# An adaLN attention block on one core: four edits to the order of TensorE's work and to one sum of the tail

## The chip, the cores and the metric

The kernel runs on 1 core of one Trainium2 chip. The metric is the device time of the whole program in microseconds (us), lower is better. The engines are TensorE (PE; its weight loads are PEld), VectorE (DVE), ScalarE (ACT), GpSimd (POOL) and SyncE (SP), which issues most DMAs.

## The reference

Two batches of 256 tokens, width 1152, all bf16. A modulation vector from c scales and shifts a layer norm of x; one attention head over the full width follows; a gate and x close the block.

```python
def reference(x, c, wqkv, wo, w_mod):        # x 2x256x1152, c 2x1152
    mod = (_silu(c) @ w_mod).reshape(B, 6, 1, D)
    shift_a, scale_a, gate_a = mod[:, 0], mod[:, 1], mod[:, 2]   # the rest is unused
    h = _layernorm(x, axis=-1) * (1 + scale_a) + shift_a
    q, k, v = split(h @ wqkv, 3)
    p = _softmax(einsum('bqd,bkd->bqk', q, k) * D ** (-0.5), axis=-1)
    a = einsum('bqk,bkd->bqd', p, v) @ wo
    return x + gate_a * a
```

## The kernel before

There are T = 512 tokens in TT = 4 tiles of 128 (tiles 0 and 1 are batch 0, tiles 2 and 3 batch 1), and the width is KT = 9 blocks of 128. The order of the instructions on PE, DVE, ACT and SP's queue is the order in which the program records them: the helpers `ten`, `vec`, `sca` and `spq` note every instruction, and `pin` at the end ties each to the one before it. All of them are therefore shown under one line, L76, in the profile, and are told apart by their tiles. POOL's instructions keep program order too. PSUM has two pools: `psum` with six slots (tag "mm") and `psum_pre` with two (tag "pre"). A slot passes to the next tile of its tag when the tile in it has been read for the last time.

The stages, in order of PE's work:

1. **Start.** Eleven filler matmuls (`fillers`, tile junk_ps) run while the first loads are under way. c is turned into silu(c), repeated along columns in scT_rep. DVE and ACT normalise x (xn), PE transposes xn (`transposes(t, h)`: h = 0 is blocks 0 to 3, KA = 4 of them, h = 1 is blocks 4 to 8), and ACT or DVE copies the result to xnT (`xnT_copy`).
2. **Scale, first column part.** `scale_block` multiplies wS, the scale columns of w_mod, with silu(c), one 128-column block j of the output and one of the nine blocks kk of the input at a time. For the first KA = 4 output blocks the result lies in psSA, one PSUM bank, which a matmul of ones fills with the 1 of (1 + scale). DVE's `scaled(k, b, ...)` multiplies block k of xnT for batch b with it into hTs; s1p holds the values for later use.
3. **Half steps.** `qkv_half(k, b)` adds block k of batch b to six accumulators accs (the first 768 columns of wqkv, from wA): six matmuls of 256 columns. They stand between the transposes of tiles 3 and 2.
4. **Scale, second column part.** psSB collects the remaining five output blocks (45 matmuls of 54 columns), DVE adds 1 into s1p and makes ten scaled tiles. Then `qkv_step(4)` to `qkv_step(8)`, six matmuls of 512 columns each for both batches, with the shift blocks (wH, bankH) and a seventh accumulator between them, and the shift's part through wqkv as a bias.
5. **The other columns of Q and K**: 11 groups of nine 512-column matmuls from hT, weights wq_t. DVE meanwhile builds the gate (gacc from wG); POOL sums it over the partitions (gate_bc).
6. **Scores**, then V: `v_group(gidx)`, twelve groups of nine 384-column matmuls, each emptied into v_sb by ACT or DVE. The softmax (DVE, ACT) yields pn for each batch.
7. **P's transposes**: eight transposes into two "pre" tiles pT_ps, copied to pT by DVE (batch 0) and ACT (batch 1); then attention, 36 matmuls of 256 columns, into attnT.
8. **Output.** For each token tile, three 384-column chunks of nine matmuls with wO. DVE multiplies with gate_bc (ga) and adds x (o_sb), and SP sends the tile out. The last tile's last 384 columns are cut into 320 and 64. For them POOL has multiplied wo with the gate beforehand (wo_last, nine products, L572), and x enters through PE by an identity matmul at the head of the chunk; DVE copies the 320 columns out, ACT the 64, and ACT's queue sends these.

The loads are issued by SP in a fixed order: c, two tiles of x, wS's first part in five pieces, wA for blocks 0, 1 to 2 and 3, wS's second part in two pieces, wA for blocks 4 to 5 and 6 to 8, wH in five pieces, then the other weights. wG takes wS's place in SBUF, wO takes wH's.

Of the kernel before, what the change touches and what calls it, by code (L numbers as in the profile page):

```python
# [8 lines left out]
ALU = mybir.AluOpType  # L9
AX = mybir.AxisListType  # L10
F32 = mybir.dt.float32
# [5 lines left out]
def kernel(  # L17
# [10 lines left out]
    P = 128  # L28
    B, N, D = x.shape
    T = B * N  # L30
    KT = D // P
    TT = T // P
    NQ = N // P
    CW = 384
    NCH = D // CW
# [6 lines left out]
    KA = 4  # L42
    CA = KA * P
    NRS = 96
    NRH = 54
# [14 lines left out]
    psum_pre = ctx.enter_context(tc.tile_pool(name="psum_pre", bufs=2, space=PSUM))  # L60
# [22 lines left out]
    vec = _Rec(nc.vector, dve_seq)  # L83
    sca = _Rec(nc.scalar, act_seq)
    ten = _Rec(nc.tensor, pe_seq)

    def pin(seq):
# [11 lines left out]
        out=ident, in_=ident, compare_op=ALU.not_equal, fill=1.0, base=0,  # L99
# [4 lines left out]
    ones_bf = const.tile([P, P], BF16)  # L104
    nc.gpsimd.memset(ones_bf, 1.0)
    ones_row = const.tile([1, 512], BF16)
# [9 lines left out]
    x_sb = act.tile([P, TT, D], BF16)  # L116
# [29 lines left out]
    wS = wmpool.tile([P, KT, D], BF16, tag="wS")  # L146
# [25 lines left out]
    def fillers(n):  # L172
        for jj in range(n):
            ten.matmul(junk_ps, lhsT=ident, rhs=junk_rhs, start=True, stop=True)
# [8 lines left out]
        out=scT_f.rearrange("p k b -> p b k"),  # L183
        in0=cT_ps.rearrange("p (b k) -> p b k", b=B),
        in1=e_sb.rearrange("p (b k) -> p b k", b=B),
        op=ALU.mult,
# [4 lines left out]
    def sc_rhs(kk, n):  # L191
        return scT_rep[:, kk].rearrange("p r b -> p (r b)")[:, 0:n]
# [17 lines left out]
    def dve_norm(t):  # L210
        vec.scalar_tensor_tensor(
            out=nb[:, t : t + 1], in0=mv_all[:, t, 0:1], scalar=-1.0, in1=rstd[:, t : t + 1],
            op0=ALU.mult, op1=ALU.mult,
        )
        vec.tensor_scalar(
            out=xn[:, t, :], in0=x_sb[:, t, :], scalar1=rstd[:, t : t + 1], scalar2=nb[:, t : t + 1],
            op0=ALU.mult, op1=ALU.add,
        )
# [22 lines left out]
    def transposes(t, h, pool, tag):  # L241
        k0, k1 = HALF[h]
        tp = pool.tile([P, KH, P], BF16, tag=tag, name="tp")
        for k in range(k0, k1):
            ten.transpose(tp[:, k - k0, :], xn[:, t, k * P : (k + 1) * P], ident)
        tps[t, h] = tp

    def xnT_copy(t, h, on_dve):
        k0, k1 = HALF[h]
        dst, srct = xnT[:, k0:k1, t * P : (t + 1) * P], tps[t, h][:, : k1 - k0, :]  # L250
        if on_dve:
            vec.tensor_copy(out=dst, in_=srct)
        else:
            sca.copy(out=dst, in_=srct)


    s1p = const.tile([P, KT, B], F32)
# [1 line left out]
    sh_bf = const.tile([P, KT, B], BF16)  # L259
    hTs = act.tile([P, KT, T], BF16, tag="a3")  # L260

    psSA = psum_pre.tile([P, KA, NRS], F32, tag="pre")
    ten.matmul(psSA.rearrange("p j r -> p (j r)"), lhsT=ones_bf[0:1, :],
               rhs=ones_row[0:1, 0 : KA * NRS], start=True, stop=False, skip_group_check=True)
    fillers(N_JUNK - 6)

    def scale_block(ps_, n, k0, k1, kk, ones=True):
        for j in range(k0, k1):
            ten.matmul(
                ps_[:, j - k0, :], lhsT=wS[:, kk, j * P : (j + 1) * P], rhs=sc_rhs(kk, n),  # L270
                start=(kk == 0 and j == k0 and not ones), stop=(kk == KT - 1), skip_group_check=True,
            )

    def scaled(k, b, scalar):
        sl = slice(b * N, (b + 1) * N)
        vec.tensor_scalar(out=hTs[:, k, sl], in0=xnT[:, k, sl], scalar1=scalar, scalar2=None, op0=ALU.mult)

    def qkv_half(k, b):
        sl = slice(b * N, (b + 1) * N)
        for f in range(NACC):  # L280
            ten.matmul(
                accs[f][:, sl], lhsT=wA[:, k, f * P : (f + 1) * P], rhs=hTs[:, k, sl],
                start=(k == 0 and b == 0), stop=False, skip_group_check=True,
            )
# [30 lines left out]
    dve_norm(1)  # L315
    dve_stats(2, 0)
    dve_norm(0)
    scale_block(psSA, NRS, 0, KA, 0)
    scale_block(psSA, NRS, 0, KA, 1)
    transposes(1, 0, psum, "mm")  # L320
    transposes(1, 1, psum, "mm")
    xnT_copy(1, 0, False)
    xnT_copy(1, 1, False)
    scale_block(psSA, NRS, 0, KA, 2)
    scale_block(psSA, NRS, 0, KA, 3)
    transposes(0, 0, psum, "mm")
    transposes(0, 1, psum, "mm")
    xnT_copy(0, 0, False)
# [3 lines left out]
    dve_aggr(2)  # L332
    act_norm(3)
    for kk in range(4, KT):
        scale_block(psSA, NRS, 0, KA, kk)

    accs = []
    for f in range(NACC):
        acc_t = psum.tile([P, T], F32, tag="mm")
        accs.append(acc_t)  # L340

    scaled(0, 0, psSA[:, 0, 0:1])
    vec.tensor_copy(out=s1p[:, 0:KA, :], in_=psSA[:, :, 0:B])
    for k in range(1, KA):
        scaled(k, 0, s1p[:, k, 0:1])
    dve_norm(2)
    qkv_half(0, 0)
    qkv_half(1, 0)
    qkv_half(2, 0)
    transposes(3, 0, psum_pre, "pre")  # L350
    xnT_copy(3, 0, False)
    transposes(2, 0, psum_pre, "pre")
    xnT_copy(2, 0, True)
    qkv_half(3, 0)
    transposes(3, 1, psum_pre, "pre")
    xnT_copy(3, 1, False)
    for k in range(KA):
        scaled(k, 1, s1p[:, k, 1:2])
    for k in range(3):
        qkv_half(k, 1)  # L360
    transposes(2, 1, psum_pre, "pre")
    xnT_copy(2, 1, True)
    psSB = psum_pre.tile([P, KT - KA, NRH], F32, tag="pre")
    for kk in range(KT):
        scale_block(psSB, NRH, KA, KT, kk, ones=False)
    vec.tensor_scalar_add(out=s1p[:, KA:KT, :], in0=psSB[:, :, 0:B], scalar1=1.0)
    for k in range(KA, KT):
        for b in range(B):
            scaled(k, b, s1p[:, k, b : b + 1])
    qkv_half(3, 1)  # L370


# [103 lines left out]
    for f in range(NB, 2 * KT):  # L476
        wt, off = w_cols(f * P, P)
        ps = psum.tile([P, T], F32, tag="mm")
# [37 lines left out]
    N_V_EARLY = 4  # L516

    def v_group(gidx):
        t, vc = divmod(gidx, NCH)
        wv_t, wv_off = w_cols(2 * D + vc * CW, CW)  # L520
        ps = psum.tile([P, CW], F32, tag="mm")
        for k in range(KT):
            ten.matmul(
                ps, lhsT=hT[:, k, t * P : (t + 1) * P], rhs=wv_t[:, k, wv_off : wv_off + CW],
                start=(k == 0), stop=(k == KT - 1),
            )
        evac(1 if gidx < N_V_EARLY else gidx, v_sb[:, t, vc * CW : (vc + 1) * CW], ps)
# [24 lines left out]
    SYNC_SCHED = mybir.DependencyInfo(mybir.DependencyClass.Sync, mybir.DependencyReason.SCHED_ONLY)  # L552
    tc.add_manual_dep(gate_ars[B - 1].ins, dve_seq[-1].ins.name, SYNC_SCHED, reason="keep gpsimd off the shared port")

    for gidx in range(N_V_EARLY, TT * NCH):
        v_group(gidx)

    attnT = act.tile([P, KT, T], BF16, tag="a2")
    pT_sbs = []
    for b in range(B):  # L560
        pT_ps = psum_pre.tile([P, NQ, N], BF16, tag="pre")
        for i in range(NQ):
            for j in range(NQ):
                ten.transpose(pT_ps[:, j, i * P : (i + 1) * P], pns[b][:, i, j * P : (j + 1) * P], ident)
        pT = work.tile([P, NQ, N], BF16, tag="pT")
        evac(b, pT, pT_ps)
        pT_sbs.append(pT)
    LASTW = 64
    TAILW = CW
    wo_last = const.tile([P, KT, TAILW], BF16)  # L570
# [16 lines left out]
    for t in range(TT):  # L587
        b = t // NQ
        o_sb = work.tile([P, D], BF16, tag="o_sb")
        if t < TT - 1:  # L590
            chunks = [(oc * CW, CW) for oc in range(NCH)]
            dma_after = {NCH - 1: (0, D)}
        else:
            chunks = [(0, CW), (CW, CW), (2 * CW, CW - LASTW), (D - LASTW, LASTW)]
            dma_after = {1: (0, 2 * CW), 2: (2 * CW, CW - LASTW), 3: (D - LASTW, LASTW)}
        for ci, (c0, w_) in enumerate(chunks):
            cs = slice(c0, c0 + w_)
            last = (t == TT - 1) and (ci == len(chunks) - 1)
            pregated = (t == TT - 1) and c0 >= D - TAILW
            ps = psum.tile([P, w_], F32, tag="mm")  # L600
            if pregated:
                ten.matmul(ps, lhsT=ident, rhs=x_sb[:, t, cs], start=True, stop=False)
            for k in range(KT):
                ten.matmul(
                    ps, lhsT=attnT[:, k, t * P : (t + 1) * P],
                    rhs=(wo_last[:, k, c0 - (D - TAILW) : c0 - (D - TAILW) + w_] if pregated else wo_k[k][:, cs]),
                    start=(k == 0 and not pregated), stop=(k == KT - 1),
                )
            if last:
                sca.copy(out=o_sb[:, cs], in_=ps)  # L610
            elif pregated:
                vec.tensor_copy(out=o_sb[:, cs], in_=ps)
            else:
                ga = work.tile([P, CW], F32, tag="ga")
                vec.tensor_tensor(out=ga[:, :w_], in0=ps, in1=gate_bc[:, b, cs], op=ALU.mult)
                vec.tensor_tensor(out=o_sb[:, cs], in0=ga[:, :w_], in1=x_sb[:, t, cs], op=ALU.add)
            if ci in dma_after:
                d0, dw = dma_after[ci]
                dma_eng = nc.scalar if last else spq
                dma_eng.dma_start(out=out_f[t * P : (t + 1) * P, d0 : d0 + dw], in_=o_sb[:, d0 : d0 + dw])  # L620
# [35 lines left out]
```

## Time and profile before

| what | us |
|---|---|
| median of 3 runs (lowest, highest) | 101.91 (101.87, 102.03) |
| the profiled execution's own time | 102.05 |
| its span, first to last instruction | 100.3 |
| PE busy in the span | 92.7 (92%) |
| DVE, ACT, POOL busy | 72.3, 31.5, 29.0 |

The profile is one execution. Its view by stages cuts the span into stretches and adds up how long each engine was busy in each; the granted clock of TensorE is 1.00 in every one from 7 us on. PE stands still within the stages from 12.33 to 19.48 (busy 7.03 of 7.15) and 74.36 to 75.27 (0.62 of 0.91), and not at all between 19.48 and 74.36. A matmul's recorded end is modelled and lies behind the start of the next one, so recorded idle time of PE is shorter than the time in which it could have started something. DMA is busy until about 57 us and nearly idle behind that.

### The profile page before, as it was taken

To read this page: it belongs to the slowest core of one execution; us is meant where nothing else is said; L and a number is where in the kernel's file an instruction comes from. 1 tells how busy PE (TensorE), PEld (TensorE's weight loads), DVE (VectorE), ACT (ScalarE), POOL (GpSimd) and SP (SyncE) were. 2 spreads that over 40 slices of the span, in tenths; PEclk is the share of its full clock that TensorE was granted. 3 is DMA by queue.
4 is the path that set the end of the run, shared out by engine and by line. 5 is a ranking of instruction groups with operands and counts; after the bars stand their busy time and mean duration, and the time that the engine had idled before them with its cause. 6 is when DMAs were issued, how large, how long until landed. Compare 5 with 4: busy or idle time off the path is not lost.

```text
span 100.3 us, 1871 instructions
## 1 busy us (share of the span) xinstructions
PE 92.7 (92%) x767; PEld 57.0 (57%) x767; DVE 72.3 (72%) x131; ACT 31.5 (31%) x62; POOL 29.0 (29%) x29
## 2 busy tenths in 40 slices
PE   0987799999999999999999999999999999999970
PEld 0236698745667444444448865656658765656550
DVE  1699732730169999999999999955636767989860
ACT  5478822000139954223322022146225400000000
POOL 5037300000000000000899000000898002999700
PEclk9999999999999999999999999999999999999999
DMA  2999999999999999999999910000000000303212
GB/s 48 359 297 315 391 368 376 384 394 390 349 362 349 363 384 346 305 319 326 326 365 394 371 38 0 0 0 0 7 0 0 0 0 0 118 7 117 86 70 80
DMA packets 16963, 21.06 MB, mean 210 GB/s; under 512 B 827, under 2 KB 12603, under 8 KB 16955
## 3 DMA queue, kind: packets, MB, share of 16 engines
q1 hardware_dynamic: 16523, 20.34, 60.2%
q10 hardware_dynamic: 432, 0.61, 2.1%
q8 instruction: 6, 0.10, 0.5%
q14 instruction: 2, 0.02, 0.1%
HBM read 19.76 MB, written 1.18 MB: 209 GB/s over the span
## 4 chain that ended last, share of the span: by engine, by line
PE 83%; DMA 11%; DVE 1%; SPq 1%; issue 0%; ACT 0%
PE ps L76 61%; PE acc_t L76 11%; DMA wA<-in_wqkv_dram 6%; DMA x_sb<-in_x_dram 5%; PE s_ps L76 4%; PE bankH L76 4%; PE acc_last L76 2%; PE psSB L76 1%; PE tp L76 1%; SPq L76 1%; DVE hTs L76 0%; DVE pT L76 0%; PE pT_ps L76 0%; ACT o_sb L76 0%; DVE s1p L76 0%
## 5 line engine op out<-in xcount | busy, mean ns | idle before, releaser
L498 POOL PARTITION_ALL_REDUCE gate_bc<-gacc x2 | 14.1, 7068 | 51.7 <-DVE gacc L76 36.5
L76 DVE SCALAR_TENSOR_TENSOR gacc<-wG,scT_f,gacc 128x1152 f32<-128x1152 bf16 x16 | 27.4, 1714 | 0.6
L76 PE MATMUL ps<-hT,wq_t 128*128 128x512 bf16 x99 | 21.5, 379 | 0.0
L76 PE MATMUL ps<-wq_t,hT 128*128 128x384 bf16 x108 | 17.7, 326 | 0.0
L76 PE MATMUL ps<-wO,attnT 128*128 128x384 bf16 x99 | 16.3, 326 | 0.0
L76 PEld LDWEIGHTS <-wq_t 128*128 128x128 bf16 x99 | 9.6, 98 | 11.4
L76 PEld LDWEIGHTS <-attnT 128*128 128x128 bf16 x117 | 10.9, 98 | 6.7
L76 PEld LDWEIGHTS <-hT 128*128 128x128 bf16 x108 | 10.6, 98 | 6.9
L76 PE MATMUL acc_t<-hTs,wA 128*128 128x256 bf16 (+1 forms) x78 | 13.0, 313 | 0.7 <-DVE hTs L76 0.5
L76 PEld LDWEIGHTS <-wA 128*128 128x128 bf16 x150 | 9.6, 96 | 5.2 <-DMA wA<-in_wqkv_dram 0.8
L572 POOL TENSOR_TENSOR wo_last<-wO,gate_bc 128x384 bf16<-128x384 bf16 x9 | 10.1, 1153 | 7.2 <-issue 7.2
L76 ACT CAST qkT<-ps 128x512 bf16<-128x512 f32 x11 | 6.3, 589 | 12.0 <-PE ps L76 12.0
L76 DVE TENSOR_TENSOR ga<-ps,gate_bc 128x384 f32<-128x384 f32 x11 | 6.1, 553 | 2.8 <-PE ps L76 2.8
L76 DVE TENSOR_TENSOR o_sb<-ga,x_sb 128x384 bf16<-128x384 f32 x11 | 7.8, 709 | 0.4
L76 ACT CAST v_sb<-ps 128x384 bf16<-128x384 f32 x8 | 3.7, 480 | 11.6 <-PE ps L76 11.6
L76 DVE COPY acc_sb<-acc_t 128x512 f32<-128x512 f32 x2 | 1.3, 685 | 6.3 <-PE acc_t L76 6.3
L76 ACT CAST o_sb<-ps 128x64 bf16<-128x64 f32 x1 | 0.2, 212 | 17.4 <-PE ps L76 17.4
L76 DVE BATCH_NORM_STATS2 stats<-x_sb 128x6 f32<-128x384 bf16 x9 | 4.5, 542 | 0.7 <-DMA x_sb<-in_x_dram 0.7
L76 ACT COPY acc_sb<-acc_t 128x512 f32<-128x512 f32 x2 | 1.1, 588 | 11.2 <-PE acc_t L76 11.2
L76 ACT COPY xnT<-tp 128x512 bf16<-128x512 bf16 (+1 forms) x6 | 3.6, 641 | 2.7 <-PE tp L76 2.7
L76 PE MATMUL ps<-pT,v_sb 128*128 128x256 bf16 x36 | 4.1, 272 | 0.3 <-DVE pT L76 0.3
L76 DVE CAST attnT<-ps 128x512 bf16<-128x512 f32 (+1 forms) x6 | 3.5, 602 | 1.1 <-PE ps L76 1.1
(79 smaller groups left out, 88.1 us busy)
## 6 DMA issues: line engine op xcount, KB each, us to landing
wq_t<-in_wqkv_dram SPq DMA_DIRECT2D x5, 864.0 KB, 10.7
wG<-in_w_mod_dram SPq DMA_DIRECT2D x3, 864.0 KB, 10.7
wO<-in_wo_dram SPq DMA_DIRECT2D x3, 864.0 KB, 9.7
wH<-in_w_mod_dram SPq DMA_DIRECT2D x4, 576.0 KB, 11.7
wS<-in_w_mod_dram SPq DMA_DIRECT2D x4, 256.0 KB, 5.8
wA<-in_wqkv_dram SPq DMA_DIRECT2D x2, 448.0 KB, 7.9
wq_t<-in_wqkv_dram SPq DMA_DIRECT2D x3, 288.0 KB, 10.8
out_dram<-o_sb SPq DMA_DIRECT2D x3, 288.0 KB, 2.1
```

The lines of the kernel that those rows point to most:

```text
L76: r = fn(*a, **k)
L498: ar = nc.gpsimd.partition_all_reduce(gate_bc[:, b, :], gacc[:, b, :], P, bass.bass_isa.ReduceOp.add)
L572: nc.gpsimd.tensor_tensor(out=wo_last[:, k, :], in0=wo_k[k][:, D - TAILW :], in1=gate_bc[:, B - 1, D - TAILW :], op=ALU.mult)
```

## The change

Four edits, in the order of the program:

- The first output block of the scale (j = 0) gets a tile of its own, psS0, in the second "pre" slot; psSA keeps the blocks 1 to 3. Each has its matmul of ones (96 and 288 columns), and psS0's comes behind the fillers. The first scaled tile reads psS0; a second small DVE copy brings psS0 into s1p.
- Between the half steps the transposes of tiles 3 and 2 are put elsewhere. The second column part of the scale (45 matmuls, the addition of 1, the ten scaled tiles) now stands ahead of qkv_half(2, 1) and qkv_half(3, 1), where it stood between them.
- P's eight transposes and their two copies stand ahead of the twelfth group of V instead of behind it.
- In the last tile's 320-column chunk the identity matmul is gone, and DVE adds x while it empties the chunk. The 64-column chunk stays as it was.

```diff
-    psSA = psum_pre.tile([P, KA, NRS], F32, tag="pre")
+    psSA = psum_pre.tile([P, KA - 1, NRS], F32, tag="pre")
     ten.matmul(psSA.rearrange("p j r -> p (j r)"), lhsT=ones_bf[0:1, :],
-               rhs=ones_row[0:1, 0 : KA * NRS], start=True, stop=False, skip_group_check=True)
+               rhs=ones_row[0:1, 0 : (KA - 1) * NRS], start=True, stop=False, skip_group_check=True)
     fillers(N_JUNK - 6)
+    psS0 = psum_pre.tile([P, NRS], F32, tag="pre")
+    ten.matmul(psS0, lhsT=ones_bf[0:1, :], rhs=ones_row[0:1, 0:NRS], start=True, stop=False,
+               skip_group_check=True)
+    def scale_A(kk):      # as scale_block(psSA, NRS, 0, KA, kk), with psS0 for j == 0
...
+    def scale_B(kk):      # as scale_block(psSB, NRH, KA, KT, kk, ones=False)
...
-    scaled(0, 0, psSA[:, 0, 0:1])
-    vec.tensor_copy(out=s1p[:, 0:KA, :], in_=psSA[:, :, 0:B])
+    scaled(0, 0, psS0[:, 0:1])
+    vec.tensor_copy(out=s1p[:, 1:KA, :], in_=psSA[:, :, 0:B])
     for k in range(1, KA):
         scaled(k, 0, s1p[:, k, 0:1])
+    vec.tensor_copy(out=s1p[:, 0, :], in_=psS0[:, 0:B])
     dve_norm(2)
     qkv_half(0, 0)
     qkv_half(1, 0)
-    qkv_half(2, 0)
     transposes(3, 0, psum_pre, "pre")
     xnT_copy(3, 0, False)
+    qkv_half(2, 0)
     transposes(2, 0, psum_pre, "pre")
     xnT_copy(2, 0, True)
-    qkv_half(3, 0)
     transposes(3, 1, psum_pre, "pre")
     xnT_copy(3, 1, False)
+    qkv_half(3, 0)
     for k in range(KA):
         scaled(k, 1, s1p[:, k, 1:2])
-    for k in range(3):
-        qkv_half(k, 1)
+    qkv_half(0, 1)
+    qkv_half(1, 1)
     transposes(2, 1, psum_pre, "pre")
     xnT_copy(2, 1, True)
     psSB = psum_pre.tile([P, KT - KA, NRH], F32, tag="pre")
     for kk in range(KT):
-        scale_block(psSB, NRH, KA, KT, kk, ones=False)
+        scale_B(kk)
     vec.tensor_scalar_add(out=s1p[:, KA:KT, :], in0=psSB[:, :, 0:B], scalar1=1.0)
     for k in range(KA, KT):
         for b in range(B):
             scaled(k, b, s1p[:, k, b : b + 1])
+    qkv_half(2, 1)
     qkv_half(3, 1)
...
-    for gidx in range(N_V_EARLY, TT * NCH):
+    for gidx in range(N_V_EARLY, TT * NCH - 1):
         v_group(gidx)
...
         pT_sbs.append(pT)
+    v_group(TT * NCH - 1)
...
-            if pregated:
+            if last:
                 ten.matmul(ps, lhsT=ident, rhs=x_sb[:, t, cs], start=True, stop=False)
...
-                    start=(k == 0 and not pregated), stop=(k == KT - 1),
+                    start=(k == 0 and not last), stop=(k == KT - 1),
...
             elif pregated:
-                vec.tensor_copy(out=o_sb[:, cs], in_=ps)
+                vec.tensor_tensor(out=o_sb[:, cs], in0=ps, in1=x_sb[:, t, cs], op=ALU.add)
```

More of the change, by code (lines that the diff above doesn't have):

```diff
@@ L260 @@
     hTs = act.tile([P, KT, T], BF16, tag="a3")
-    psSA = psum_pre.tile([P, KA, NRS], F32, tag="pre")
+    psSA = psum_pre.tile([P, KA - 1, NRS], F32, tag="pre")
     ten.matmul(psSA.rearrange("p j r -> p (j r)"), lhsT=ones_bf[0:1, :],
-               rhs=ones_row[0:1, 0 : KA * NRS], start=True, stop=False, skip_group_check=True)
+               rhs=ones_row[0:1, 0 : (KA - 1) * NRS], start=True, stop=False, skip_group_check=True)
     fillers(N_JUNK - 6)
-    def scale_block(ps_, n, k0, k1, kk, ones=True):
-        for j in range(k0, k1):
-            ten.matmul(
-                ps_[:, j - k0, :], lhsT=wS[:, kk, j * P : (j + 1) * P], rhs=sc_rhs(kk, n),
-                start=(kk == 0 and j == k0 and not ones), stop=(kk == KT - 1), skip_group_check=True,
+    psS0 = psum_pre.tile([P, NRS], F32, tag="pre")
+    ten.matmul(psS0, lhsT=ones_bf[0:1, :], rhs=ones_row[0:1, 0:NRS], start=True, stop=False,
+               skip_group_check=True)
+    def scale_A(kk):
+        for j in range(KA):
+            ten.matmul(
+                psS0 if j == 0 else psSA[:, j - 1, :], lhsT=wS[:, kk, j * P : (j + 1) * P], rhs=sc_rhs(kk, NRS),
+                start=False, stop=(kk == KT - 1), skip_group_check=True,
+            )
+    def scale_B(kk):
+        for j in range(KA, KT):
+            ten.matmul(
+                psSB[:, j - KA, :], lhsT=wS[:, kk, j * P : (j + 1) * P], rhs=sc_rhs(kk, NRH),
+                start=(kk == 0 and j == KA), stop=(kk == KT - 1), skip_group_check=True,
             )
@@ L317 @@
     dve_norm(0)
-    scale_block(psSA, NRS, 0, KA, 0)
-    scale_block(psSA, NRS, 0, KA, 1)
+    scale_A(0)
+    scale_A(1)
     transposes(1, 0, psum, "mm")
@@ L323 @@
     xnT_copy(1, 1, False)
-    scale_block(psSA, NRS, 0, KA, 2)
-    scale_block(psSA, NRS, 0, KA, 3)
+    scale_A(2)
+    scale_A(3)
     transposes(0, 0, psum, "mm")
@@ L334 @@
     for kk in range(4, KT):
-        scale_block(psSA, NRS, 0, KA, kk)
+        scale_A(kk)
     accs = []
```

## The prediction

> **What bounds the kernel now.** First the page: how busy each engine is, and who holds the chain that ended last.
>
> ```profile
> PE 92.7 (92%) x767; PEld 57.0 (57%) x767; DVE 72.3 (72%) x131; ACT 31.5 (31%) x62; POOL 29.0 (29%) x29
> PE 83%; DMA 11%; DVE 1%; SPq 1%; issue 0%; ACT 0%
> ```
>
> TensorE (PE) is the bound, and DMA holds the chain only ahead of 12.3 us. So an edit pays only where PE stands still behind 12.3 us, or where it takes work off PE. Second view, the chain in order of time, at those places:
>
> ```profile
> 6.18 6.10 DMA wA<-in_wqkv_dram
> 12.28 0.05 issue
> 12.33 1.48 PE acc_t L76 x12
> ...
> 17.57 1.15 PE psSB L76 x45
> 18.72 0.02 issue
> 18.74 0.18 DVE s1p L76
> 18.92 0.03 issue
> 18.95 0.49 DVE hTs L76 x2
> 19.44 0.04 issue
> 19.48 4.04 PE acc_t L76 x18
> ...
> 74.53 0.24 PE pT_ps L76 x4
> 74.77 0.02 issue
> 74.79 0.43 DVE pT L76
> 75.22 0.04 issue
> 75.27 21.84 PE ps L76 x155
> 97.11 0.02 issue
> 97.13 0.21 ACT o_sb L76
> ```
>
> The chain leaves PE twice, for DVE: at 18.72 (second scale block, s1p, two scaled tiles, step 4) and at 74.77 (P's transposes, copy, attention). Third view, PE's own timeline at the tail, which shows the identity matmul that the change removes (start, duration):
>
> ```profile
> 95.28 0.30 PE L76 MATMUL ps<-x_sb,ident 128*128 128x320 bf16 x1
> 95.42 1.39 PE L76 MATMUL ps<-wo_last,attnT 128*128 128x320 bf16 x9
> 96.64 0.19 PE L76 MATMUL ps<-x_sb,ident 128*128 128x64 bf16 x1
> ```
>
> A matmul's recorded end lies behind the start of the next one, so I count PE from start to start: 0.109 us for 256 columns (18 half-step matmuls from 15.17 to 17.13), 0.056 for a transpose (8 from 13.65 to 14.10), 0.0252 in the second scale block (45 from 17.41 to 18.54), 0.1625 for 384 columns (108 in 17.55), 0.136 for 320 (10 from 95.28 to 96.64).
>
> **Second scale block ahead of two half steps.** Before, only qkv_half(3,1) stands between the block and step 4: it starts at 18.54, takes 6 x 0.109 = 0.655 and leaves PE idle from 19.195 to 19.48, 0.285. The DVE path needs 19.48 - 18.54 = 0.94 from the block's last issue. Now twelve matmuls, 1.31, stand there, so the gap closes with 0.37 to spare: **-0.285**. The block itself comes 0.655 earlier, and its loads must have landed. The second part of wS (640 KB, issued at 8.30, 8.6 to landing) is there at 16.9; its first use moves to 17.41 - 0.655 + 25 x 0.0252 = 17.39. wA for step 4 (issued at 9.11, longest wA landing 9.7) is there at 18.8, used at 19.20. Both hold by 0.4 to 0.5. If such a load were later, PE would stand with the half steps queued behind the block, and 0.285 is what would go first.
>
> **P's transposes ahead of V's last group.** Before: eight transposes from 74.36 to 74.81, then PE waits until 75.27 for DVE's 0.42 copy: 0.455. After: transposes at 72.90 to 73.35, V's last group (9 x 0.1625 = 1.46) to 74.81, attention at once: **-0.455**. The cover: DVE empties the group before from 73.10 for 0.56, then copies P until about 74.1, 0.7 ahead of need; without V's group the old wait would be back. The transposes now stand at the head of PE's queue with V's group behind them, and wait for the softmax: its last pn ends at 69.75 + 0.62 = 70.37, 2.5 early. ACT copies the second P (0.58) before it empties V's last group (0.48), finished near 75.5; attention reads that group in batch 1, from 74.81 + 18 x 0.109 = 76.77. No wait is late next.
>
> **x added on VectorE.** One 320-column identity matmul less: **-0.136** on PE, right before the end. DVE's copy becomes an add. The trace has no add of this shape. Its nearest row is ga<-ps,gate_bc (one PSUM, one SBUF operand), 553 ns for 384 elements, and a DVE copy of 384 (v_sb<-ps) has 550, so two operands cost what one does and I take the copy's own 0.49 for 320; nothing suggests less. The upper bound is an o_sb row stretched to 1.17. DVE was idle 0.21 before that copy; with PE 0.136 earlier 0.07 remains, so its start moves with PE. The last chunk keeps its identity matmul, its ACT copy (97.13) and its DMA (97.37 + 1.8 to landing); DVE's DMA lands 0.16 earlier (97.35 + 1.7), so ACT's path stays the end.
>
> **The first scale block's own bank.** psS0 ends three matmuls before psSA; at 0.042 each (20 in 0.84) hTs and the first half step could start 0.125 earlier. But the second half step's weights say:
>
> ```profile
> 12.32 0.11 PEld L76 LDWEIGHTS <-wA 128*128 128x128 bf16 x2 [0.41 <-DMA wA<-in_wqkv_dram]
> ```
>
> PE waits there for a load that lands at 12.28 whatever PE did before. **0**; bounds -0.125 (if that load were early) and +0.16 (the extra DVE copy, the s1p row's 0.16, if it delayed something). That copy only delays xn of tile 2, from 12.81 to 12.97; its transposes come at 13.87. The extra 96-column ones matmul (0.042) runs before wS lands at 7.16, where PE idles 0.42.
>
> **Transposes of tiles 3 and 2 between the half steps.** The same 13 transposes and 12 matmuls in another order: 0. The third group now needs ACT's copy of the first one: its last transpose starts at 13.16 and lasts 0.22, then 0.04 and the copy's 0.58, 14.00, against PE's arrival at 14.10. If that cover fails by up to 0.14 it is absorbed: at 15.03 PE waits 0.14 for the scaled tiles anyway.
>
> No DMA and no POOL instruction changes its place. wG's first load reuses wS and so waits for the second scale block, which only ends earlier; it is issued at 22.23, long after.
>
> **Does the gain carry?** From 19.48 to 74.36 PE is busy without a break (in the view by stages 12.02 of 12.02, 21.40 of 21.40, 3.90 of 3.90), and DVE, ACT and softmax are fed by PE, so they move with it. Loads do not. The tightest is the third weight chunk for K: issued at 29.90, at most 12.5 to landing, 42.4, needed at 31.52 + 54 x 0.2167 = 43.2, now 42.9. POOL moves by 0.285 only, since it follows the softmax, while the tail moves by 0.74. Its nine wo_last products run from 84.53 for 10.07, to 94.60 (94.32 then); the last is needed by the ninth matmul of the 320 chunk, at 96.50 before and 95.62 then: 1.3 spare.
>
> The tail's DVE work does meet POOL 0.455 longer. While POOL multiplies, o_sb rows last 0.62 to 1.17 instead of 0.56; ga rows stay at 0.54 to 0.56. If the last tile's first o_sb (now from 93.87) takes 1.17, then ga, o_sb and three hand-overs of 0.035 bring DVE to the final add at 96.25 instead of 95.96, and its DMA lands 0.29 - 0.16 = 0.13 behind ACT's. Bounds 0 and +0.13; I take +0.03, since only that one o_sb can be hit and POOL must be in the wrong phase for it.
>
> The Trainium skill speaks against the change here: its page "SBUF — State Buffer", section "SBUF: two separate sides", holds that GpSimd and a VectorE operation with two SBUF inputs lock each other out for a whole instruction. By it an o_sb may wait out a full product (0.91) and last 1.47, DVE would be 0.59 late, and the sum -0.45 (an estimate from that page); the add itself, with one input in PSUM, would not be locked out. No o_sb of this trace is that long.
>
> Sum: -0.285 - 0.455 - 0.136 + 0.03 = -0.85. On the profiled execution (102.05, span 100.3) that is 101.20. The median of the runs, 101.91, lies 0.14 below the profiled one; taking the same from it gives **101.06**.
>
> **Rivals.**
> A load bounds the second scale block or step 4. For it: 0.4 spare, with DMA busy all through. Against it: both landings are read off. The 0.285 is lost: 101.35. Chance 0.08.
> The tail turns to DVE: contention with POOL or a slower add takes 0.1 to 0.25 back: 101.15 to 101.3. Chance 0.10.
> P's wait moves elsewhere (softmax late, V's last group late for batch 1), giving back 0.455: 101.5. Against it are 2.5 and 1.2 us spare. Chance 0.04.
> The edits do nothing, because the gaps belong to something that is late anyway: 101.9. Against it is the unbroken PE behind each gap. Chance 0.03.
> Slower: TensorE's clock is granted later. The first six filler matmuls run at 0.427 us, the next five at 0.218, so the full clock came near 5.4; the change re-cuts the ones matmuls among these fillers. At half clock the stretch behind 12.33 costs half its length: the gain of 0.85 is gone if the clock comes only at 12.33 + 1.7 = 14.0, and at 16 the time is 101.06 + 1.8 = 102.9. Against it: the fillers are the same eleven, and PE waits for loads until 12.3 anyway. Chance 0.03. The Trainium skill, "TensorE: Matmul & The Clock Gate", Part 1, describes a free-running window of about 3.4 us; by that figure the steps after 5.4 are 8.8, 12.2 and 15.6, and only the last would hurt (an estimate from that page).
>
> **How the numbers follow.** The likeliest case has 0.72; its own range is 100.93 to 101.2 (all of part one's 0.125 to a tail of +0.14). With the tail and load cases the range is 100.93 to 101.38, which holds 0.85 or so. Faster by over 0.2% (0.2 us, about what a measurement here can tell) in the first four cases: 0.94; same 0.03; slower 0.03.
>
> **What would show it.** Right: no DVE step in the chain near 18.7 and 74.8, attention right behind V's last group, nine matmuls of 320 columns at the tail, and the load of wA still ahead of the second half step. Wrong: a PE wait for wS or wA between 16.7 and 19.2, o_sb rows over 0.6 in the last tile with DVE's DMA last, or filler matmuls at 0.427 behind 5.4.

## The result, and the profile after

The changed kernel takes 101.39 us (median of 20 runs, 101.11 to 102.56), the kernel before 102.27 in 20 runs that include the three of the front page (101.87 to 102.86): a ratio of 0.9924 [0.9899, 0.9950], faster. The profiled execution took 101.25 with a span of 99.5, where the one before took 102.05 with 100.3. The forecast was 101.06, range 100.93 to 101.38: the time lies 0.01 above the range. The forecast saving of 0.85 agrees with the measurement: 0.85 of 101.91 is a ratio of 0.9917, inside the interval, which reaches from 0.51 to 1.03 us. What failed is the level from which the saving was taken.

The page first:

```profile
PE 93.0 (93%) x767; PEld 57.1 (57%) x767; DVE 72.3 (73%) x132; ACT 31.6 (32%) x62; POOL 29.1 (29%) x29
PE 84%; DMA 11%; SPq 1%; issue 0%; ACT 0%
```

DVE is gone from the second line, the shares of the chain. Its place shows in the chain in order of time (start, duration, what):

```profile
6.30 6.05 DMA wA<-in_wqkv_dram
12.34 0.05 issue
12.39 0.83 PE acc_t L76 x6
...
16.98 1.13 PE psSB L76 x45
18.11 5.20 PE acc_t L76 x30
...
72.84 0.45 PE pT_ps L76 x8
73.29 23.01 PE ps L76 x163
96.30 0.02 issue
96.32 0.21 ACT o_sb L76
```

In this view the chain never leaves PE between 12.39 and ACT's last copy. The second scale block is followed by 30 matmuls in one piece (two half steps and three steps) where s1p and the scaled tiles stood, and P's transposes by V's last group and attention, 163 matmuls in one piece, where DVE's pT copy stood. From the start of half step (1, 0) to the start of ACT's last copy it is 96.32 - 12.39 = 83.93, against 97.13 - 12.33 = 84.80 before: **-0.87**. The three closed gaps were forecast at 0.285 + 0.455 + 0.136 = 0.876. The second load of wA landed 0.06 later, at 12.34, and the span is therefore only 0.81 shorter.

The tail, as the timeline has it (start, duration; in brackets idle time and what ended it):

```profile
93.94 0.56 DVE L76 TENSOR_TENSOR o_sb<-ga,x_sb 128x384 bf16<-128x384 f32 x1
...
95.40 0.56 DVE L76 TENSOR_TENSOR o_sb<-ga,x_sb 128x384 bf16<-128x384 f32 x1
...
96.03 0.49 DVE L76 TENSOR_TENSOR o_sb<-ps,x_sb 128x320 bf16<-128x320 f32 x1
96.32 0.21 ACT L76 CAST o_sb<-ps 128x64 bf16<-128x64 f32 x1 [17.23 <-PE ps L76]
```

The add took the 0.49 that the copy had taken, DVE was idle 0.07 ahead of it, and both of the last tile's o_sb (from 93.94 and 95.40) took 0.56. And the first half steps, in the view of weight loads:

```profile
12.39 0.11 PEld L76 LDWEIGHTS <-wA 128*128 128x128 bf16 x2 [0.57 <-DMA wA<-in_wqkv_dram]
```

The first half step starts 0.10 earlier than before (11.28 for 11.38), the wait for wA behind it grew from 0.41 to 0.57, and the second half step starts when the load is there.

### The profile page after: what moved, and what is told of

It reads as the page before. It is cut to its first block, busy times and chain, and to the rows that moved or that the text cites. A ratio compares the mean times of both kernels' runs of the same rounds, so it can differ in the third digit from the quotient of the medians.

```text
span 99.5 us, 1872 instructions
## 1 busy us (share of the span) xinstructions
PE 93.0 (93%) x767; PEld 57.1 (57%) x767; DVE 72.3 (73%) x132; ACT 31.6 (32%) x62; POOL 29.1 (29%) x29
## 4 chain that ended last, share of the span: by engine, by line
PE 84%; DMA 11%; SPq 1%; issue 0%; ACT 0%
PE ps L76 61%; PE acc_t L76 11%; DMA wA<-in_wqkv_dram 6%; DMA x_sb<-in_x_dram 5%; PE s_ps L76 4%; PE bankH L76 4%; PE acc_last L76 2%; PE psSB L76 1%; PE tp L76 1%; SPq L76 1%; PE pT_ps L76 0%; ACT o_sb L76 0%
## 5 line engine op out<-in xcount | busy, mean ns | idle before, releaser
L76 PE MATMUL junk_ps<-junk_rhs,ident 128*128 128x512 bf16 x11 | 4.8, 605 | 0.0
```

The source lines that it names most:

```text
L76: r = fn(*a, **k)
```

## The experiments

Two times are read from each trace: when half step (1, 0) starts, and the **stretch** from there to the start of ACT's last copy. Times in us; the ratio is to the kernel before, run on the same chip. Counted to the last matmul instead, as in some of the expectations, every stretch is 0.23 shorter.

| kernel | half step (1, 0) | stretch | span | median | ratio [95%] |
|---|---|---|---|---|---|
| before | 12.33 | 84.80 | 100.27 | | 1 |
| after | 12.39 | 83.93 | 99.46 | 101.39 | 0.9924 [0.9899, 0.9950] |
| e1_block | 12.39 | 84.73 | 100.25 | 102.01 | 0.9994 [0.9965, 1.0023] |
| e2_ptrans | 12.47 | 84.34 | 100.04 | 101.67 | 0.9956 [0.9936, 0.9976] |
| e3_tailadd | 12.37 | 84.67 | 100.19 | 102.00 | 0.9987 [0.9961, 1.0013] |
| e4_bank | 12.30 | 85.35 | 100.79 | 102.30 | 1.0013 [0.9994, 1.0033] |
| e10_fill_before | 12.61 | 84.52 | 100.28 | 102.06 | 0.9989 [0.9958, 1.0021] |
| e11_fill_after | 12.27 | 84.05 | 99.46 | 101.37 | 0.9919 [0.9874, 0.9963] |
| e12_fill_t2 | 12.63 | 83.79 | 99.56 | 101.37 | 0.9908 [0.9874, 0.9942] |
| e13_fill_t2_split | 11.82 | 84.42 | 99.39 | 101.42 | 0.9933 [0.9901, 0.9965] |
| e7_late | 13.31 | 83.93 | 100.36 | 101.85 | 0.9963 [0.9939, 0.9987] |
| e14_all | 11.75 | 84.36 | 99.25 | 100.97 | 0.9864 [0.9840, 0.9888] |
| e15_nosplit | 12.36 | 83.79 | 99.29 | 101.21 | 0.9897 [0.9871, 0.9923] |
| e16_all_nobank | 11.94 | 83.79 | 98.86 | 100.73 | 0.9848 [0.9823, 0.9873] |

The kernel before had medians of 102.09 (34 runs, with e1 to e4), 102.10 (25, with e10 to e13) and 102.24 (17, with the rest).

### Each edit alone, on the kernel before

**e1_block**: the second scale block one half step earlier.

```diff
-    for k in range(3):
-        qkv_half(k, 1)
+    qkv_half(0, 1)
+    qkv_half(1, 1)
...
+    qkv_half(2, 1)
     qkv_half(3, 1)
```

> Only the second scale block moved ahead of two half steps; all else as before. Theory (the parts add on PE): the idle 0.285 us between the last half step and step 4 closes, so the time is 0.29 below before (ratio 0.997), and in the profile step 4 starts 0.109 behind the last half step. Rival (a load of wS or wA bounds the moved block): PE idles at the block or at step 4, gain under 0.1.

Its ratio cannot be told from 1, nor from the forecast 0.997. Step 4's weight load, in the timeline of weight loads:

```profile
19.45 0.33 PEld L76 LDWEIGHTS <-wA 128*128 128x128 bf16 x3 [0.31 <-DMA wA<-in_wqkv_dram]
```

The DVE path is covered, but in this execution wA for step 4 landed at 19.40 and not at 18.83 as in the profile of before. PE had issued its last half-step matmul at 19.15 and could have gone on at 19.26; it did at 19.45, so 0.19 of the 0.285 came back as a wait for that load. This is the rival "a load bounds step 4", in part.

**e2_ptrans**: P's transposes ahead of V's last group.

```diff
-    for gidx in range(N_V_EARLY, TT * NCH):
+    for gidx in range(N_V_EARLY, TT * NCH - 1):
...
         pT_sbs.append(pT)
+    v_group(TT * NCH - 1)
```

> Only P's transposes moved ahead of V's last group. Theory: attention follows V's last group at once, 0.455 below before (ratio 0.9955). Rival (the wait moves to the softmax or to V's last group): PE idles ahead of P's transposes or in attention's batch 1, gain under 0.2.

The stretch is 0.46 shorter and the ratio 0.9956 is 0.45 of 102.09. PE's timeline has transposes, V's group and attention without a gap:

```profile
73.04 0.61 PE L76 MATMUL pT_ps<-ident,pn 128*128 128x128 bf16 x8
73.48 1.63 PE L76 MATMUL ps<-wq_t,hT 128*128 128x384 bf16 x9
74.95 0.49 PE L76 MATMUL ps<-pT,v_sb 128*128 128x256 bf16 x3
```

In this execution the second load of wA landed early, at 11.88, and half step (1, 0) followed the first one without a wait, 0.14 later than before. What came late was the first half step, at 11.82 (11.38 before). The chain says why:

```profile
0.75 3.78 DMA x_sb<-in_x_dram
4.53 0.02 issue
4.56 1.49 DVE stats L76 x3
...
11.47 0.30 DVE hTs L76
11.78 0.04 issue
11.82 2.13 PE acc_t L76 x18
```

ACT's first load of x landed at 4.53 (4.10 before), and the 0.43 went on by way of DVE's normalisation, the transposes and the scaled tile.

**e3_tailadd**: the identity matmul gone, x added by DVE.

```diff
-            if pregated:
+            if last:
                 ten.matmul(ps, lhsT=ident, rhs=x_sb[:, t, cs], start=True, stop=False)
...
-                vec.tensor_copy(out=o_sb[:, cs], in_=ps)
+                vec.tensor_tensor(out=o_sb[:, cs], in0=ps, in1=x_sb[:, t, cs], op=ALU.add)
```

> Only the 320-column chunk's identity matmul replaced by DVE's add. Theory: 0.136 below before (ratio 0.9987), DVE's add 0.49 long, ACT's DMA still the last. Rival (DVE becomes the last): the add lasts 0.55 or more or starts late, DVE's DMA lands last, gain 0 to 0.05.

The stretch is 0.13 shorter, and the ratio 0.9987 is 0.13 as well, but its interval reaches 0.27 to either side: the runs alone cannot tell the gain from none. The add takes 0.49, as in the changed kernel.

**e4_bank**: psS0 with its own bank, order as before.

```diff
-    psSA = psum_pre.tile([P, KA, NRS], F32, tag="pre")
+    psSA = psum_pre.tile([P, KA - 1, NRS], F32, tag="pre")
...
+    psS0 = psum_pre.tile([P, NRS], F32, tag="pre")
...
-    scaled(0, 0, psSA[:, 0, 0:1])
+    scaled(0, 0, psS0[:, 0:1])
```

> Only the first scale block in a bank of its own. Theory: the first half step starts 0.125 earlier, the second one still waits for its load of wA near 12.3, and the time is that of before (0). Rival (the first half step is what counts): 0.12 below before. Over all four profiles of this call, the theory that the level of a run is set by that load expects the span to follow the load's landing one for one, once each edit's own gain is taken off; the rival is that the levels differ where the landings do not.

No gain. The first half step starts 0.20 earlier (11.18); PE idles 0.33 ahead of it instead of 0.46, so 0.13 of this is the bank's. The second starts at 12.30, when the load is there. The stretch is 0.55 longer for a reason that the edit does not touch:

```profile
18.54 0.54 PEld L76 LDWEIGHTS <-wS 128*128 128x128 bf16 x19 [0.48 <-DMA wS<-in_w_mod_dram]
```

In this execution wS's second part landed at 18.50 (16.95 before), and PE stood 0.53 in the middle of the second scale block, at 18.01, where the landing of before would have left 1.06 to spare. Its time, 102.60, is at the upper end of its runs (101.87 to 102.68, median 102.30): here a high run has a trace, and the cause in it is one late load.

As for the level of a run, the first four profiles do not bear out that the load ahead of half step (1, 0) sets it. Only e3_tailadd's span follows that landing. e1_block lost 0.19 and e4_bank 0.53 to other loads behind it, and e2_ptrans did not wait for it at all.

### Another way to close the gap ahead of step 4

**e10_fill_before** leaves the scale block of before where it was, and puts three matmuls that need no new load into the gap: the first part of the seventh accumulator (`last_acc(0, 3)`).

```diff
+    accs.append(psum_pre.tile([P, T], F32, tag="pre", name="acc_last"))
     bankH = psum_pre.tile([P, 512], F32, tag="pre")
...
-    accs.append(psum_pre.tile([P, T], F32, tag="pre", name="acc_last"))
+    last_acc(0, 3)
     qkv_step(4)
...
-    last_acc(0, 3)
```

> The kernel before, with the idle 0.285 us ahead of step 4 filled from the other side: the second scale block stays where it was, and the first three matmuls of the seventh accumulator (last_acc(0, 3), 3 x 0.2165 = 0.65 us, no load needed) move from behind the fourth shift block to between the last half step and step 4; the two tiles of the small PSUM pool swap their slots for it. No load is needed earlier than before. Theory (moving the block ahead paid little on its own, 0.9994, because its load and step 4's are needed earlier and land late in some runs): this order gains the full 0.285, ratio 0.997, and step 4 shows no wait for wA. Rival (that idle time is given back later on PE whatever fills it): ratio 0.999 to 1.000, with a new PE wait behind step 4.

The stretch is 0.28 shorter: the gap is closed without asking for wS any earlier. The span is unchanged because the load landed 0.28 later, at 12.56:

```profile
6.14 6.42 DMA wA<-in_wqkv_dram
12.56 0.05 issue
...
18.98 0.65 PE acc_t L76 x6
19.64 0.65 PE acc_last L76 x3
20.28 3.88 PE acc_t L76 x18
```

Over its runs the ratio, 0.9989, decides nothing between 0 and 0.28.

**e11_fill_after** does the same in the changed kernel, with the scale block back behind three half steps:

```diff
-    qkv_half(0, 1)
-    qkv_half(1, 1)
+    for k in range(3):
+        qkv_half(k, 1)
...
-    qkv_half(2, 1)
     qkv_half(3, 1)
...
+    last_acc(0, 3)
     qkv_step(4)
```

**e12_fill_t2** also moves tile 2's first transposes ahead of qkv_half(2, 0), to close the 0.14 at 15.0.

```diff
-    qkv_half(2, 0)
     transposes(2, 0, psum_pre, "pre")
     xnT_copy(2, 0, True)
+    qkv_half(2, 0)
```

> The changed kernel, with the second scale block put back behind three half steps and the same filler ahead of step 4. Theory: as fast as the changed kernel's best runs and less often slow, 0.87 to 0.9 below before (ratio 0.9913), against 0.9924 for the changed kernel. Rival (the order of the block made no difference to the late runs): ratio that of the changed kernel, with the same upper runs above 102.2.

> The kernel e11_fill_after with the transposes of tile 2's first half moved ahead of half step (2, 0), so that DVE's copy and the scaled tiles of batch 1 come 0.65 us earlier. Theory: the idle 0.137 us ahead of half step (0, 1), which stands in both kernels, closes: 1.0 below before (ratio 0.990). Rival (the next load takes its place): PE waits 0.1 or more in the second scale block or at step 4.

e11's stretch holds a wait of 0.10 for the third chunk of K's weights (wq_t); without it, it is 83.95, that of the changed kernel. e12's is 83.79, 0.14 shorter than the changed kernel's: the gap closed, as forecast. In both, wA for step 4 landed late (19.46 and 19.35), and PE did not wait for it: the three filler matmuls put the need 0.65 later. Both medians are 101.37: the changed kernel's time to within the intervals. That e11 is less often slow is not shown: one of its seven runs took 102.44, and three of the changed kernel's twenty took over 102.2.

### When the second load of wA lands

**e7_late** swaps two loads of the changed kernel, and nothing else.

```diff
-    load_wA(1, 3)
     load_wA(3, KA)
+    load_wA(1, 3)
```

> The changed kernel with wA's second and third load swapped in SP's queue (blocks 1 to 2 behind block 3): the load that half step (1, 0) waits for lands about 0.6 later, near 12.95. Theory (the level of a run is set one for one by that landing): the stretch from half step (1, 0) to the last matmul stays at 83.70 as in the changed kernel, and the time rises by 0.55 to 0.6, to 0.998 of before. Rival (slack further on takes it up): the stretch shrinks by 0.2 or more.

The load landed 0.92 later, at 13.26; half step (1, 0) started at 13.31, and the stretch behind it is 83.93, the same to 0.01:

```profile
13.31 0.33 PEld L76 LDWEIGHTS <-wA 128*128 128x128 bf16 x4 [1.19 <-DMA wA<-in_wqkv_dram]
```

So in this execution the landing sets the end one for one. Of the 0.92, the swap accounts for some 0.57: the first load of wA and both parts of wS's second column part, which the swap leaves in their places, landed 0.35 late too. The median moved by 0.46 (ratio 0.9963 against 0.9924), where 0.55 to 0.6 was forecast.

**e13_fill_t2_split** halves the load, on e12, so that half step (1, 0) waits for block 1 alone.

```diff
-    load_wA(1, 3)
-    load_wA(3, KA)
+    load_wA(1, 2)
+    load_wA(2, KA)
```

> The kernel e12_fill_t2 with wA's second load cut to block 1 alone and block 2 joined to block 3 (pieces 0, 1, 2 to 3 instead of 0, 1 to 2, 3), no more loads than before. Theory (PE's start is set by the landing of wA's second load near 12.3, one for one): that piece lands 0.6 earlier, half step (1, 0) follows the first one at once, near 11.9, and the own bank of the first scale block pays its 0.125 for the first time; the time falls by 0.3 to 0.45, ratio 0.986. Rival (the next loads bound PE anyway): PE waits for wA at half step (2, 0) or for wS in the second scale block, gain under 0.1 against e12_fill_t2.

Half step (1, 0) starts 0.57 earlier than in the changed kernel, and the span is 0.07 shorter. The ratio is 0.9933, where 0.986 was forecast: no gain over e12 is shown. The stretch gave the rest back, to loads that PE had not waited for in the changed kernel: from start to start 0.09 at step 4, 0.24 at a shift block, 0.25 at the third K weight chunk:

```profile
25.64 0.24 PEld L76 LDWEIGHTS <-wH 128*128 128x128 bf16 x7 [0.19 <-DMA wH<-in_w_mod_dram]
42.86 0.11 PEld L76 LDWEIGHTS <-wq_t 128*128 128x128 bf16 x2 [0.58 <-DMA wq_t<-in_wqkv_dram]
```

### Versions that beat both

Two orders address those two waits: qkv_step(8) ahead of the last two early shift blocks, and wG's last load behind the third K weight chunk instead of the second. **e14_all** is e13 with both, **e15_nosplit** e12 with both (the load whole), **e16_all_nobank** e14 without psS0 (psSA holds four blocks again).

```diff
+    qkv_step(8)
     shift_block(4)
     shift_block(5)
-    qkv_step(8)
...
         if i == 1:
             load_mod(wG, 2, 3, 6, 0, D)
+        if i == 2:
             load_mod(wG, 2, 6, KT, 0, D)
```

> The kernel e13_fill_t2_split with two changes of order against its new waits: the third weight chunk of K is loaded ahead of the gate's last blocks (wG 6 to 8), and step 8 stands ahead of the shift blocks 4 and 5, whose load lands near 25.5. Theory (each of the waits seen there was for one load): from half step (1, 0), near 11.85, to the last matmul 83.6 to 83.7, so 1.5 below before, ratio 0.985. Rival (loads as a whole bound PE up to 43 us): the waits move on to other loads and the ratio stays at 0.990 or above.

> The same two changes of order on e12_fill_t2, that is without the cut of wA's second load. Theory: the stretch is 83.56, half step (1, 0) waits for its load again (12.2 to 12.6), ratio 0.990. Rival: faster than e14_all, because more loads in time behind outweigh the earlier start.

> The kernel e14_all without the own bank of the first scale block: psSA holds all four blocks again. Theory: where no load stands ahead of half step (1, 0), the own bank is worth three matmuls, 0.125, so this is 0.12 slower than e14_all and half step (0, 0) starts 0.12 later. Rival (the first scaled tile does not wait for the last three matmuls): no difference.

e14 and e16, with the split load, beat both kernels: their intervals lie under that of the changed one. e15's overlaps it. e14's 0.9864 and e15's 0.9897 are near their forecasts. In e14's profile step 4 waits:

```profile
19.61 0.33 PEld L76 LDWEIGHTS <-wA 128*128 128x128 bf16 x3 [0.76 <-DMA wA<-in_wqkv_dram]
```

That load landed at 19.57; in e16's at 19.06, and no load was waited for behind the half steps. So e16, expected to lose what its first half step starts later (11.29 for 11.10), came out lower. The two intervals overlap, and whether the own bank is worth anything in time stays open.

## Why the prediction was wrong

**The step that failed** is the last of the sum: "The median of the runs, 101.91, lies 0.14 below the profiled one; taking the same from it gives 101.06". The profiled execution came out at 101.25 against 101.20; the load that landed 0.06 later accounts for the difference. But the median of 20 runs lies 0.14 *above* that execution, not below. So the term -0.14 measured +0.14: with it, 0.28 of the 0.33 by which the forecast missed, and the load makes the other 0.05. Likewise the three runs of before (101.87 to 102.03) lie at the bottom of what the same kernel does: 101.87 to 102.86 over 20 runs, and no later series of it has a median under 102.09. From 102.27 the same 0.85 gives 101.42; 101.39 was measured. Three close runs were taken as a narrow distribution.

**The range left out** what moves one execution against another. It reached up only by way of the rivals, and held nothing for the landing of wA near 12.3, which the prediction itself had named as the start of the chain. Over the ten profiles in which that load was neither cut nor swapped, it landed between 11.88 and 12.58, and half step (1, 0) started between 12.27 and 12.63. By e7_late's one-for-one that is 0.36 of width, against a range of 0.45; late loads further on add up to 0.53 in single executions (e4_bank). Why the timed runs differ stays open: in every run whose span is on record the time is 1.7 to 1.9 longer than the span, so the scatter lies inside the span, but only the profiled runs have a trace. Of these, e4_bank's shows a late load behind a high time.

**Second scale block, -0.285.** Right in the profile after, where the chain runs through; only an upper value otherwise. The prediction gave the loads 0.4 to 0.5 to spare, read from one trace. Over all 14 profiles wS's second part landed at 16.55 to 17.35, and once at 18.50; wA for step 4 landed at 18.47 to 19.57, in six of them behind 19.26. The needs were 17.39 and 19.20 (19.26 in the profile after). So the margin for step 4 is smaller than the scatter, and the rival given 0.08 is a thing of single executions: e1_block lost 0.19 to it, and e14_all, which reaches step 4 about as early, 0.43. The whole change's runs do not show a loss, so its mean size stays open.

**P's transposes, -0.455**, and **the tail's add, -0.136**, held in the traces, at 0.46 and 0.13 alone; with the second scale block they make up the 0.87. **The tail's contention, +0.03**, was 0 in the profile after, and partly by luck. POOL's products started 0.70 earlier and not the 0.285 that was forecast, because the idle time ahead of them was shorter too:

```profile
83.83 10.12 POOL L588 TENSOR_TENSOR wo_last<-wO,gate_bc 128x384 bf16<-128x384 bf16 x9 [6.75 <-issue]
```

It was 7.23 before, with the start at 84.53, and over the 14 profiles it lies anywhere from 6.75 to 7.80. So o_sb met POOL as it had, and none was over 0.6 in the last tile. In e2_ptrans, where the idle time was 7.80 and the products ran until 95.11, the last tile's first o_sb was hit:

```profile
94.30 1.23 DVE L76 TENSOR_TENSOR o_sb<-ga,x_sb 128x384 bf16<-128x384 f32 x1
```

There DVE had no idle time left ahead of its last copy, but ACT's DMA still landed last, at 98.98 against 98.82. That tail has the identity matmul; what a hit of that length costs with DVE's add no run shows.

**The own bank, 0**: right, by the reason given. **The transposes, 0**: right, though they were not run alone. The 0.137 near 15.0 stayed, and from half step (1, 0) to the second scale block it is 5.08 in both profiles, when the half step that moved behind the block is added back.

**The slower rival's sign appeared** and cost nothing: the profile after has fillers at half clock behind 5.4,

```profile
5.60 2.08 PE L76 MATMUL junk_ps<-junk_rhs,ident 128*128 128x512 bf16 x5
```

and the granted clock is full from 7.32 instead of 5.43, but PE waits for loads until 12.39 anyway. The change is not the reason: e1_block and e2_ptrans, which keep the fillers of before, have it full from 7.14 and 8.43. Even the 8.43 cost nothing that the trace shows, since e2_ptrans's chain comes to PE only at 9.83.

## What to carry to other kernels

A saving read off a trace from start to start can be good to 0.01 us, but a forecast in microseconds is no better than the level it starts from: three runs that agree say little about the spread of twenty, so give the level its own width, and the ratio as the claim. Judge the margin of a load against the scatter of its landings, not against the one landing that the trace shows; work that is pulled ahead into a gap needs its load earlier, while filling the gap with work that needs no new load does not. The runs here show no difference between the two (e11_fill_after 0.9919, the changed kernel 0.9924). After each shortening look for the load that is late next: here the earlier start of e13 showed no gain until the two orders behind it were changed too.

## What the runs showed of the hardware

- The landing of one load varies between executions: wS's second part at 16.55 to 17.35 in 13 profiles and 18.50 in one, wA for step 4 at 18.47 to 19.57. In e4_bank's trace 15 of wS's 16 completions were in by 16.9, the last at 18.50. Of wA for step 4 the fifteenth came at 17.72 to 18.42 in all profiles, and the last 0.11 to 1.48 behind it: one straggler sets the landing. Which engine it is and why stays open.
- The full clock of TensorE came between 5.43 and 8.43 us with the same or nearly the same fillers ahead of it.
- An add of one PSUM and one SBUF operand took DVE what a copy from PSUM took: 0.49 for 320 columns.
- POOL's idle time between its sum over partitions and the first of its products is 6.75 to 7.80 us over the 14 profiles, with nothing in the profile that it waits for.
